# A fused attention, expert and gating kernel: lower weight halves a step later, masks ahead of ranks, last rows stored from ScalarE's queue

## The chip, the core and the metric

The kernel runs on one core of a Trainium2 chip. A core has TensorE (PE, matmuls; PEld is its weight load), VectorE (DVE), ScalarE (ACT), GpSimd (POOL) and SyncE (SP, which here only issues DMAs). ScalarE and GpSimd can issue DMAs too. Every engine works through its own list of instructions in order; semaphores hold an instruction until what it needs is there. The metric is the device time of one execution in microseconds (us), taken as the median of several runs; one more execution is profiled, and its trace is what the rows below come from.

## What is computed

Three layers follow one another: a linear attention with decay, a mixture of experts with one expert per token, and a gated projection. Cut to what matters:

```python
# attention, blocks of 64 positions, per head a decay lam
intra = (qb @ kb.T * Dmask) @ vb                  # Dmask[i, j] = lam ** (i - j) for i >= j, else 0
out   = intra + (qb * lam_pow) @ kv_state
kv_state = lam ** 64 * kv_state + (kb * rev_pow).T @ vb
# experts: x is [2, 768, 512]
for b, s:                                         # in order of s
    fresh = argmax(x[b, s] @ w_gate)
    e = fresh if s == 0 or sigmoid(x[b, s] @ w_local) < 0.5 else e_of_the_token_before
    p = softmax(x[b, s] @ w_gate)
    out[b, s] = p[e] * (relu(x[b, s] @ w1[e]) @ w2[e])
# gated projection: causal convolution of 5 taps, sigmoid gate
out = (sigmoid(conv(x)) * (x @ w_val)) @ w_out
```

## The kernel before, in words

There are 12 groups of 128 tokens (`NT`; 6 per batch entry) and 8 experts. The program has three parts.

**Attention and routing.** A loop over `s` from 2 to 11 pipelines four groups: `s`, `g1 = s-1`, `g2 = s-2`, `g3 = s-3`. In a step TensorE makes the scores of `s` (`scores`, L291), the attention output of `g1` (`mix_state` L309, `mix` L317), its next state (`next_state`, L346), then turns that output and multiplies it with the gate's weights (`turned`, L366 to L371); it also turns the expert choices of `g2` (`choice_turned` L427, `experts_turned` L439) and counts tokens per expert (`counted` L451, `counted_rest` L454, `indices` L469). VectorE masks the scores (`mask`, L298, two instructions), picks the expert (`logits` L376, `choice` L410 to L412), runs the scan along the tokens (`experts`, L435), ranks tokens within their expert (`ranks` L458, `index_factors` L463), and makes queries, states and half of the scaled keys. ScalarE copies the attention output (`mixed`, L323), the gate results (`token_rows`, L382 and L384), scaled keys (`keys`, L271), the one-hot rows (`one_hots`, L444 to L446), and at the end of a group its softmax (`softmax`, L420); after it the group's token rows (128 rows of 520 numbers, `xtok`) are stored to the DRAM table `xd` (L421).

In the same loop expert 0's first weights are prepared. A float32 weight tile is split into two parts that TensorE multiplies in its faster float32 form: the upper half is a cast on ScalarE (`split_hi`, L177), the lower half is the raw tile less the upper half on VectorE (`split_lo`, L181). `first_load(n)` (L171) loads raw tile `n` on SP's queue; `first_hi` and `first_lo` split half a tile (512 columns) per step, tiles 0 to 3 in steps 4 to 11. The raw tiles share four buffers, so that a load waits until the split of an older tile is done.

**The attention's end.** After the loop the last groups (`ge` = 9, `g0` = 10, `g1` = 11) go through the same steps; rows of expert 0 are not fetched from DRAM for these groups but placed by matmuls with one-hot tiles (`places` L494, `place` L502, from `xs`, the split token rows: `parts_hi` L388, `parts_lo` L391), after earlier groups' rows were gathered (`early_fetch` L482) and turned (`early_turn` L489). `early_split` (L511, L512) splits the result for expert 0.

**Experts and projection.** For each expert, `up` (L803) makes the hidden layer and `down` (L815) the output of each half of its tokens; `w1_chunk` and `w2_chunk` load and split weights ahead. The rows of expert 1 and later are gathered from `xd` by GpSimd (`x_fetch`, L759) by an index list `idx` (L672) and turned by TensorE between the two `down` calls of the expert before (`x_turn`, L779). A small gather of softmax values for expert 0 (`softmax_fetch`, L769) stands ahead of the first `x_fetch`. Every gather reads `xd`, so it needs all the stores that came before it. The gated projection follows (L1009, L1035).

The order on ScalarE, VectorE, TensorE and SP is the order in which the code is written; only GpSimd's is left to the scheduler in the first two parts. So where a call stands in the loop says where its instructions, and its DMA, stand on each queue.

Of the kernel before, what the change touches and what calls it, by code (L numbers as in the profile page):

```python
# [21 lines left out]
P = 128  # L22
# [20 lines left out]
def fused_kernel(ctx, tc, qkv, lam, wgl, w1, w2, wv, cw, wo, out, dbg=None):  # L43
# [282 lines left out]
    def decay(g):  # L326
        if 0 < g % NC < NC - 1:
            sd_t[g] = sd = at_p.tile([P, HP, D], F32, name="sdec", tag="sdec")
            for hp in range(HP):
                nc.scalar.activation(sd[:, hp, :], state[g][:, hp, :], AF.Copy, scale=lq[:, hp, P - 1:P])  # L330
# [83 lines left out]
    def inverse(g):  # L414
        den = ex_t[g][1]
        nc.vector.reciprocal(den[:, 1:2], den[:, 1:2])

    def softmax(g):
        (ex, den), xtok = ex_t.pop(g), xtok_t[g]
        nc.scalar.activation(xtok[:, DM:XW], ex, AF.Copy, scale=den[:, 1:2])  # L420
        nc.sync.dma_start(xd[1 + g * P:1 + (g + 1) * P, :], xtok)  # L421

    def choice_turned(g, b):
        fk = fk_t.pop(g)
# [96 lines left out]
    with tc.manual_schedule(engines=order_a):  # L521
        warm(10)
        scores(0, 0)
        scores(0, 1)
        mask(0)
        keys(0)
        load_qk(3)
        load_qk(4)
        scores(1, 0, True)
        scores(1, 1, True)  # L530
        mix_state(0)
        mix(0, 0)
        mix(0, 1)
        mixed(0)
        mask(1)
        keys_rest(0)
        powers()
        next_state(0)
        keep_state(0)
        queries(1)  # L540
        keys(1)
        keys_rest(1)
        scores(2, 0)
        turned(0)
        for s in range(2, NT):
            g1, g2, g3 = s - 1, s - 2, s - 3
            last = s == NT - 1
            if s < NT - 3:
                load_qk(s + 3)
            if s in (2, 4, 6, 8):  # L550
                first_load((s - 2) // 2)
            if s in (10, 11):
                first_load(s - 6)
            scores(s, 1)
            logits(g2)
            choice(g2)
            decay(g1)
            shift(g2)
            exponents(g2)
            token_rows(g2)  # L560
            if g3 >= 0:
                ranks(g3)
                index_factors(g3)
            mask(s)
            mix_state(g1)
            mix(g1, 0)
            mix(g1, 1)
            mixed(g1)
            if last:
                counted_rest(g3)  # L570
                indices(g3)
                early_fetch()
            next_state(g1)
            choice_turned(g2, g1)
            inverse(g2)
            queries(s)
            kept(g2)
            experts(g2)
            keep_state(g1)
            if not last:  # L580
                scores(s + 1, 0)
            turned(g1, (0, 1))
            experts_turned(g2)
            turned(g1, (2, 3))
            keys(s, range(2))
            one_hots(g2)
            keys_rest(s)
            keys(s, range(2, HK))
            softmax(g2)
            if last:  # L590
                parts_hi(g2)
            if s >= 4:
                first_hi((s - 4) // 2, HALF[s % 2])
                first_lo((s - 4) // 2, HALF[s % 2])
            if g3 >= 0 and not last:
                counted_rest(g3)
                indices(g3)
            counted(g2)

        ge, g0, g1 = NT - 3, NT - 2, NT - 1  # L600
        logits(g0)
        choice(g0)
        shift(g0)
        exponents(g0)
        token_rows(g0)
        parts_hi(g0)
        ranks(ge)
        places(ge)
        parts_lo(ge)
        mix_state(g1)  # L610
        mix(g1, 0)
        mix(g1, 1)
        mixed(g1)
        choice_turned(g0, g1)
        kept(g0)
        first_load(6)
        first_load(7)
        place(ge, (0,))
        parts_lo(g0)
        experts(g0)  # L620
        inverse(g0)
        turned(g1, (0, 1))
        experts_turned(g0)
        turned(g1, (2, 3))
        one_hots(g0)
        counted_rest(ge)
        counted(g0)
        place(ge, (1,))
        logits(g1)
        choice(g1)  # L630
        token_rows(g1)
        ranks(g0)
        places(g0)
        choice_turned(g1, NT)
        kept(g1)
        parts_hi(g1)
        experts(g1)
        place(g0)
        early_turn(0, (0, 1))
        experts_turned(g1)  # L640
        one_hots(g1)
        early_turn(0, (2, 3))
        counted_rest(g0)
        counted(g1)
        ranks(g1)
        places(g1)
        early_turn(1, (0, 1, 2, 3))
        parts_lo(g1)
        place(g1)
        shift(g1)  # L650
        exponents(g1)
        early_split()
        first_hi(4)
        index_factors(ge)
        index_factors(g0)
        index_factors(g1)
        inverse(g1)
        softmax(g0)
        softmax(g1)
        first_lo(4)  # L660
    idx = keep.tile([P, 2 * E], I32, name="idx")
    yslot = keep.tile([P, NT], I32, name="yslot")
# [581 lines left out]
```

## Time and profile before

| | us |
|---|---|
| runs: median of 3 (lowest, highest) | 357.74 (357.42, 358.5) |
| the profiled execution | 359.04 |
| its span, first to last instruction | 357.3 |
| busy in the span: TensorE, VectorE, ScalarE, GpSimd | 335.0, 260.5, 200.4, 66.4 |

The span is what the views cut into stretches; 1.74 us of the profiled execution lie around it. The profiled execution is 1.30 us above the median. Times in the rows count from the span's start. "Idle before" is how long an engine stood still ahead of an instruction, with what ended it. The chain of waits follows the work that ended last back to the start: at each step to what released it.

### The profile page before, as it was taken

The page shows a single profiled execution, that of the slowest core. Times are in us where ns is not written, and L with a number is a line of the kernel's source. Part 1 is how long each engine was busy: PE and PEld are TensorE (multiplying, and loading weights), DVE is VectorE, ACT ScalarE, POOL GpSimd, SP SyncE. Part 2 cuts the span into 40 slices and gives each one's busy share as a digit, 9 for nine tenths or more (in the row PEclk, how much of TensorE's full clock was granted, in tenths as well). Part 3 has the DMA queues.
Part 4 walks back from the last instruction along what each step waited for, and adds up shares of the span by engine and source line. Part 5 has one row for each costly group of instructions (what it writes and reads, how often), then busy time and mean ns, then how long its engine had stood idle before and what let it go on. Part 6 is the DMA issues. An engine that isn't in the chain of part 4 may idle for free.

```text
span 357.3 us, 6988 instructions
## 1 busy us (share of the span) xinstructions
PE 335.0 (94%) x2682; PEld 294.4 (82%) x2682; DVE 260.5 (73%) x540; ACT 200.4 (56%) x445; POOL 66.4 (19%) x89
## 2 busy tenths in 40 slices
PE   6999989979964999999999999999999999999995
PEld 2887867758943998989989889898898997999884
DVE  5777586856672788778898788776872399989880
ACT  1687577755443457564575655646552556655741
POOL 6000000020053304221241131421021263000000
PEclk9899899899996999999999999999999999999999
DMA  6988672530675778979969798797840262111012
GB/s 209 421 315 309 256 260 104 159 105 2 228 267 193 244 218 263 311 233 311 306 195 347 252 315 273 243 337 244 264 154 29 62 198 67 61 59 61 29 61 94
DMA packets 24819, 72.00 MB, mean 201 GB/s; under 512 B 3398, under 2 KB 6732, under 8 KB 23628
## 3 DMA queue, kind: packets, MB, share of 16 engines
q1 hardware_dynamic: 20020, 59.87, 49.2%
q0 software_dynamic: 2304, 7.42, 7.1%
q10 hardware_dynamic: 2456, 4.20, 3.1%
q8 instruction: 23, 0.38, 0.4%
q14 instruction: 16, 0.13, 0.1%
HBM read 57.79 MB, written 13.68 MB: 200 GB/s over the span
## 4 chain that ended last, share of the span: by engine, by line
PE 78%; DVE 7%; DMA 6%; ACT 4%; issue 1%; POOL 1%; SPq 0%; ACTq 0%; POOLq 0%; DVEq 0%
PE py L815 24%; PE ph L803 22%; PE po L1035 9%; PE pv L1009 7%; PE ps L291 3%; PE po L317 2%; DMA xr<-xd,idx 2%; PE rt L366 2%; DMA qk<-in_qkv_dram 2%; DMA xd<-xtok 2%; DVE sm L298 2%; DVE whl L181 1%; PE px L779 1%; DVE gt L995 1%; PE po L309 1%
## 5 line engine op out<-in xcount | busy, mean ns | idle before, releaser
L181 DVE TENSOR_TENSOR whl<-wraw,whl 128x1024 fp32r<-128x1024 f32 (+1 forms) x70 | 81.2, 1178 | 34.8 <-ACT whl L177 34.6
L815 PE MATMUL py<-whl,hh 128*128 128x512 f32 x384 | 93.8, 399 | 0.0
L803 PEld LDWEIGHTS ph<-xh,whl 128*128 128x128 f32 x768 | 87.3, 188 | 1.1 <-ACT xh L511 0.4
L803 PE MATMUL ph<-xh,whl 128*128 128x240 f32 x768 | 87.8, 275 | 0.2 <-ACT xh L511 0.2
L815 PEld LDWEIGHTS py<-whl,hh 128*128 128x128 f32 x384 | 71.5, 190 | 16.4
L177 ACT CAST whl<-wraw 128x1024 fp32r<-128x1024 f32 (+1 forms) x68 | 66.5, 995 | 9.2 <-DMA wraw<-in_w_dram 6.2
L806 ACT ACTIVATE hh<-ph 128x480 fp32r<-128x480 f32 x32 | 18.3, 572 | 39.2 <-PE ph L803 38.0
L995 DVE SCALAR_TENSOR_TENSOR gt<-yt,cw_sb,gt 128x256 f32<-128x256 f32 x96 | 39.0, 478 | 1.1 <-ACT gt L987 1.1
L1035 PE MATMUL po<-wo_t,gh 128*128 128x512 f32 (+1 forms) x156 | 34.6, 378 | 0.1
L1009 PEld LDWEIGHTS pv<-yh,wv_t 128*128 128x128 f32 x288 | 33.9, 188 | 0.6 <-ACT yh L972 0.2
L1009 PE MATMUL pv<-yh,wv_t 128*128 128x256 f32 x288 | 34.3, 278 | 0.0
L1035 PEld LDWEIGHTS po<-wo_t,gh 128*128 128x128 f32 x156 | 27.1, 188 | 6.0 <-DVE gh L1025 0.8
L807 DVE SCALAR_TENSOR_TENSOR hh<-ph,hh 128x480 fp32r<-128x480 f32 x32 | 21.0, 656 | 10.8 <-ACT hh L806 10.7
L291 PE MATMUL ps<-qk 64*128 64x128 f32 x176 | 19.1, 314 | 4.1 <-DVE sm L298 2.9
L822 ACT ACTIVATE yo<-py,pe 128x512 f32<-128x512 f32 x16 | 11.1, 695 | 19.1 <-PE py L815 19.1
L291 PEld LDWEIGHTS ps<-qk 64*128 64x128 f32 x176 | 13.8, 197 | 7.7 <-DVE sm L298 5.2
L759 POOL DMA_INDIRECT xr<-xd,idx x14 | 17.4, 1242 | 9.4 <-PE px L779 6.8
L271 ACT ACTIVATE kd<-qk,dm 128x64 f32<-128x64 f32 x40 | 11.4, 343 | 7.5 <-DMA qk<-in_qkv_dram 7.5
L317 PE MATMUL po<-sm,qk 128*64 128x128 f32 x192 | 15.0, 305 | 0.0
L951 POOL DMA_INDIRECT yg<-ys,yslot x10 | 11.6, 1163 | 15.9 <-DVE yh L974 11.1
L298 DVE TENSOR_TENSOR sm<-ps,dm 128x512 f32<-128x512 f32 x22 | 14.1, 682 | 0.2 <-PE ps L291 0.2
L317 PEld LDWEIGHTS po<-sm,qk 128*64 128x64 f32 x192 | 11.9, 154 | 2.4 <-issue 2.3
(172 smaller groups left out, 411.2 us busy)
## 6 DMA issues: line engine op xcount, KB each, us to landing
wraw<-in_w_dram SPq DMA_DIRECT2D x64, 512.0 KB, 5.9
qk<-in_qkv_dram SPq DMA_DIRECT2D x9, 1024.0 KB, 6.6
ys<-yo ACTq DMA_DIRECT2D x16, 256.0 KB, 6.0
xd<-xtok SPq DMA_DIRECT2D x12, 260.0 KB, 2.7
ys<-warm_sb SPq DMA_DIRECT2D x24, 128.0 KB, 5.5
out_dram<-oo SPq DMA_DIRECT2D x11, 256.0 KB, 2.0
qk<-in_qkv_dram SPq DMA_DIRECT2D x5, 512.0 KB, 8.1
wraw<-in_w_val_dram SPq DMA_DIRECT2D x4, 512.0 KB, 5.4
```

The lines of the kernel that those rows point to most:

```text
L177: nc.scalar.copy(hl[:, 0, cs], raw[:, cs])
L181: nc.vector.tensor_tensor(hl[:, 1, cs], raw[:, cs], hl[:, 0, cs].bitcast(F32), op=SUB)
L291: nc.tensor.matmul(ps_t[g][rh][:, hp, :], t[r, half, 256 + c0:256 + c0 + P], t[r, half, c0:c0 + P], start=True, stop=True)
L298: nc.vector.tensor_tensor(sm_t[g][:, rh], ps[rh], dm[:, rh * HP:(rh + 1) * HP, :], op=MUL)
L317: nc.tensor.matmul(po_t[g][hl * D:(hl + 1) * D, hp % 2, hp // 2 * P:(hp // 2 + 1) * P], qk_t[g][:, 3, h * D:(h + 1) * D], sm_t[g][:, h // ...
L803: nc.tensor.matmul(ph[:, fi, :], w1_t[e][k][:, a, f * P:(f + 1) * P], xh[:, b, k].rearrange("p t n -> p (t n)")[:, 0:C1], start=first, sto ...
L806: nc.scalar.activation(hh[:, 0, :, 0:C1], ph, AF.Relu)
L807: nc.vector.scalar_tensor_tensor(hh[:, 1, :, 0:C1], ph, 0.0, hh[:, 0, :, 0:C1].bitcast(F32), op0=ALU.max, op1=SUB)
L815: nc.tensor.matmul(py, hhs[f // 2][:, a, f % 2, t * P:(t + 1) * P], w2_t[e][f // 2][:, b, (f % 2) * DM:(f % 2 + 1) * DM], start=(n == 0), ...
L995: nc.vector.scalar_tensor_tensor(gt[:, k, :], yt[:, b, k, c0 + j:c0 + j + 256], cw_sb[:, k, j:j + 1], gt[:, k, :], op0=MUL, op1=ADD)
L1009: nc.tensor.matmul(pv[:, mi, :], wv_t[:, a, k * DM + m * P:k * DM + (m + 1) * P], yh[:, b, k, :], start=first, stop=last)
L1035: nc.tensor.matmul(po, gh[:, a, k, t * P:(t + 1) * P], wo_t[:, b, k * DM + cs.start:k * DM + cs.stop], start=(i == 0), stop=(i == 11))
```

## The change

Seven edits, all of place or queue; one line of the list of calls moves at a time, and the work itself is the same.

- In the loop the upper half of a tile is cast one step earlier (steps 3 to 10) and in the middle of the step, after `kept`; the lower half is subtracted where it was, so that it follows its upper half by a step.
- `keys(s, range(2))` comes before `experts` instead of after `turned`.
- `mask(s)` comes ahead of `ranks` and `index_factors` (except in the last step, where both come ahead of `mask`).
- `softmax` of a group, with its store, comes one step later and earlier within the step: `softmax(g3)` after `token_rows(g2)`.
- The stores of the last three groups (9, 10, 11) are issued by ScalarE, the others still by SP.
- In the attention's end `mix_state` and `mix` come ahead of the ranks, `parts_hi(g0)` comes after `kept` and `inverse`, `softmax(g0)` and `softmax(g1)` come much earlier, `parts_lo(g0)` and the placing of group 10 later and in two parts, the exponents of group 11 earlier.
- GpSimd's first gather for expert 1 comes ahead of the two small softmax gathers (the scheduler's choice).

```diff
-        nc.sync.dma_start(xd[1 + g * P:1 + (g + 1) * P, :], xtok)
+        (nc.scalar if g >= ET else nc.sync).dma_start(xd[1 + g * P:1 + (g + 1) * P, :], xtok)
...
             choice(g2)
+            if last:
+                ranks(g3)
+                index_factors(g3)
+            mask(s)
             decay(g1)
             shift(g2)
             exponents(g2)
             token_rows(g2)
             if g3 >= 0:
+                softmax(g3)
+            if g3 >= 0 and not last:
                 ranks(g3)
                 index_factors(g3)
-            mask(s)
             mix_state(g1)
...
             kept(g2)
+            if 3 <= s < 11:
+                first_hi((s - 3) // 2, HALF[(s - 3) % 2])
+            keys(s, range(2))
             experts(g2)
...
             turned(g1, (2, 3))
-            keys(s, range(2))
+            if last:
+                softmax(g2)
+                parts_hi(g2)
             one_hots(g2)
             keys_rest(s)
             keys(s, range(2, HK))
-            softmax(g2)
-            if last:
-                parts_hi(g2)
             if s >= 4:
-                first_hi((s - 4) // 2, HALF[s % 2])
                 first_lo((s - 4) // 2, HALF[s % 2])
...
         token_rows(g0)
-        parts_hi(g0)
+        mix_state(g1)
+        mix(g1, 0)
+        mix(g1, 1)
         ranks(ge)
...
         inverse(g0)
+        parts_hi(g0)
         turned(g1, (0, 1))
...
         counted(g0)
+        softmax(g0)
         place(ge, (1,))
...
         place(g1)
-        shift(g1)
-        exponents(g1)
+        inverse(g1)
+        softmax(g1)
         early_split()
         first_hi(4)
...
-        inverse(g1)
-        softmax(g0)
-        softmax(g1)
         first_lo(4)
```

On ScalarE, in one of the loop's full steps, from the copy of the attention output (`xt`) on, the list was:

```order
L323 COPY xt<-po 128x512
L431 ACTIVATE kp<-sp 8x128
L271 ACTIVATE kd<-qk,dm 128x64 x2
L444 CAST so_167<-sp 128x8
L445 COPY soall<-sp 128x8
L446 ACTIVATE so_167<-sp,tokid 128x8
L271 ACTIVATE kd<-qk,dm 128x64 x2
L420 ACTIVATE xtok<-ex,den 128x8
L177 CAST whl<-wraw 128x512
```

and in the same step it now is (`whl` is the split weight, `so_167` the one-hot rows, `kd` the scaled keys):

```order
L420 ACTIVATE xtok<-ex,den 128x8
L323 COPY xt<-po 128x512
L431 ACTIVATE kp<-sp 8x128
L177 CAST whl<-wraw 128x512
L271 ACTIVATE kd<-qk,dm 128x64 x2
L444 CAST so_167<-sp 128x8
L445 COPY soall<-sp 128x8
L446 ACTIVATE so_167<-sp,tokid 128x8
L271 ACTIVATE kd<-qk,dm 128x64 x2
```

The cast of the weight half moved from the step's last place to the middle, ahead of the one-hot rows, and the softmax from behind the keys to ahead of `xt`.

On ScalarE at the attention's end, from group 10's shift to the copy of group 11's attention output (`xt`) and beyond, the list was:

```order
L395 ACTIVATE nmx<-mx 128x1
L400 ACTIVATE ex,den<-rt,nmx 128x8
L401 ACTIVATE den<-den 128x1
L382 COPY xtok<-rt 128x256
L384 COPY xtok<-rt 128x256
L388 CAST xs<-xtok 128x512
L323 COPY xt<-po 128x512
L431 ACTIVATE kp<-sp 8x128
```

and now is:

```order
L384 COPY xtok<-rt 128x256
L323 COPY xt<-po 128x512
L431 ACTIVATE kp<-sp 8x128
L388 CAST xs<-xtok 128x512
L444 CAST so_167<-sp 128x8
L445 COPY soall<-sp 128x8
L446 ACTIVATE so_167<-sp,tokid 128x8
L420 ACTIVATE xtok<-ex,den 128x8
L421 DMA xd<-xtok 128x520
```

The split of group 10's rows (`xs`) went behind `xt` and `kp`, and the softmax with the store of `xtok` now stands here.

On SP's queue, around the two raw weight loads that stand ahead of the last stores, the difference is:

```order
 L421 DMA xd<-xtok 128x520
 L171 DMA wraw<-in_w_dram 128x1024 x2
-L421 DMA xd<-xtok 128x520 x2
 L215 DMA wraw_1595<-in_w_val_dram 128x1024
 L171 DMA wraw<-in_w_dram 128x1024 x4
```

The two stores of groups 10 and 11 no longer stand behind the two loads.

## Rows read from the trace of the kernel before

**Rows 1.** Stretches: busy PE, PEld, DVE, ACT, POOL; PE clock; DMA share; GB/s
```profile
24.85:29.95 5.10, 5.10 (x84) 4.38 (x81) 4.11 (x15) 4.31 (x21) 0.00 (x0) 1.00 0.69 215
29.95:67.53 37.58, 34.05 (x458) 28.16 (x455) 26.52 (x93) 26.60 (x116) 0.00 (x0) 0.95 0.61 221
67.53:74.03 6.50, 5.99 (x77) 4.84 (x74) 4.38 (x15) 4.48 (x22) 1.56 (x2) 0.77 0.46 127
74.03:86.53 12.50, 10.02 (x94) 8.10 (x92) 6.58 (x27) 7.01 (x28) 0.55 (x1) 1.00 0.20 63
86.53:103.40 16.87, 16.87 (x126) 15.39 (x126) 12.87 (x24) 8.38 (x13) 3.12 (x8) 1.00 0.61 211
103.40:119.20 15.80, 7.86 (x34) 6.37 (x33) 8.07 (x10) 5.22 (x7) 6.16 (x8) 0.78 0.66 215
119.20:357.30 238.10, 233.26 (x1574) 210.60 (x1572) 181.29 (x308) 131.82 (x196) 48.77 (x44) 1.00 0.59 193
```

**Rows 2.** Chain of waits through step 8: start, us, engine, what
```profile
48.84 0.19 ACT xtok L420
49.03 0.52 ACT whl L177
...
49.57 0.69 DVE whl L181
...
51.13 0.29 DVE ixa L463
51.42 1.21 DVE sm L298 x2
```

**Rows 3.** SP's first raw weight load; landing times of raw tiles, first 110 us
```profile
10.13 0.33 SPq L171 DMA_DIRECT2D wraw<-in_w_dram  x1
...
DMA to landing us min/median/max: 4.5/6.5/12.8
```

**Rows 4.** Timeline of VectorE as the attention's end begins: start, us, instruction, idle
```profile
75.10 0.69 DVE L181 TENSOR_TENSOR whl<-wraw,whl 128x512 fp32r<-128x512 f32 x1 [1.93 <-ACT whl L177]
```

**Rows 5.** Chain of waits at the attention's end
```profile
77.56 0.62 ACT xs L388
78.18 0.49 ACT xt L323
...
78.72 0.74 PE rt L366 x4
```

**Rows 6.** Timeline of ScalarE: a store that it issues itself
```profile
113.86 0.35 ACTq L824 DMA_DIRECT2D ys<-yo  x1
```

**Rows 7.** Timelines of ScalarE and SP around the last two stores
```profile
88.50 0.30 ACT L420 ACTIVATE xtok<-ex,den 128x8 f32<-128x8 f32 x1 [0.38 <-DVE den L416]
...
89.62 2.46 SPq L171 DMA_DIRECT2D wraw<-in_w_dram  x2
92.17 0.86 SPq L421 DMA_DIRECT2D xd<-xtok  x2
```

**Rows 8.** Chain of waits from the index list to expert 1's gathered rows
```profile
90.84 0.09 DVE idx L672
...
92.64 6.76 DMA xd<-xtok
...
100.18 0.95 POOL xsm L769
...
104.08 7.75 DMA xr<-xd,idx
```

**Rows 9.** All stores of token rows: landing times
```profile
DMA to landing us min/median/max: 2.1/2.7/6.8
```

**Rows 10.** Timeline of GpSimd: the second gather for expert 1
```profile
104.08 1.90 POOL L759 DMA_INDIRECT xr<-xd,idx  x1 [0.30 <-issue]
```

**Rows 11.** Timeline of TensorE, expert 1 to 2: turning, second half, next expert
```profile
135.54 0.79 PE L779 MATMUL px<-identr,xr 128*128 128x128 f32 x8
...
141.85 5.54 PE L803 MATMUL ph<-xh,whl 128*128 128x240 f32 x48
```

More of the change, by code (lines that the diff above doesn't have):

```diff
@@ L609, in fused_kernel @@
         parts_lo(ge)
-        mix_state(g1)
-        mix(g1, 0)
-        mix(g1, 1)
         mixed(g1)
@@ L618, in fused_kernel @@
         place(ge, (0,))
-        parts_lo(g0)
         experts(g0)
         inverse(g0)
+        parts_hi(g0)
         turned(g1, (0, 1))
@@ L633, in fused_kernel @@
         places(g0)
+        early_turn(0, (0, 1))
         choice_turned(g1, NT)
@@ L637, in fused_kernel @@
         experts(g1)
-        place(g0)
-        early_turn(0, (0, 1))
+        parts_lo(g0)
+        place(g0, (0,))
         experts_turned(g1)
         one_hots(g1)
+        shift(g1)
+        exponents(g1)
         early_turn(0, (2, 3))
@@ L644, in fused_kernel @@
         counted(g1)
+        place(g0, (1,))
         ranks(g1)
         places(g1)
+        parts_lo(g1)
         early_turn(1, (0, 1, 2, 3))
-        parts_lo(g1)
         place(g1)
-        shift(g1)
-        exponents(g1)
+        inverse(g1)
+        softmax(g1)
         early_split()
```

## The prediction

> **What bounds the kernel now.** I read the busy time of each stretch first, then the chain of waits inside the stretches where TensorE is not full, then the timelines around the places that the chain names. From 119.20 us to the end TensorE is busy 233.26 of 238.10 us [rows 1]: there the kernel is bound by matmuls, the change touches nothing, and whatever is won earlier should come out at the end whole. Expert 0 up to the end of its first `down` is full too (16.87 of 16.87). The stretches with holes are the six steps 5 to 10 (37.58 us, TensorE 34.05, with some of that stretched by matmuls that wait), step 11 (6.50), the attention's end (12.50, busy 10.02) and, the largest, 103.40 to 119.20, where TensorE works 7.86 of 15.80 us. The change works on exactly these four.
>
> **Steps 5 to 10.** In step 4, the last one without a weight split, TensorE is busy for 5.10 of 5.10 us [rows 1]. The next six take 37.58 / 6 = 6.26 us each. The chain shows why: it leaves TensorE and runs through ScalarE's softmax (0.19) and cast of the weight half (0.52) to VectorE's lower half (0.69), then the choice, the ranks and `ixa` (0.29) and the two masks (1.21), before TensorE may go on with the next scores [rows 2]. VectorE's next logits stand behind the lower half, which stands behind a cast that is the last thing ScalarE does in a step.
>
> With the change the lower half finds its upper half made a step earlier and waits for nothing; the softmax leaves this part of ScalarE's step; the masks no longer wait for ranks and `ixa`. What must still be done in a step is: TensorE 5.10 us, and in the six steps VectorE 26.52 / 6 = 4.42 and ScalarE 26.60 / 6 = 4.43 us [rows 1]. So TensorE should be last again, at 5.10. I take 5.30, since three engines that are each over 80% full hand work to each other in order: 6 x (6.26 - 5.30) = **5.8 us**. Ends: at 5.10 it is 7.0; if the three hold each other up and half of the 1.16 us between 6.26 and 5.10 stays, 5.68 a step, 3.5.
>
> The cast now stands ahead of the one-hot rows in ScalarE's list, and its 0.52 us are hidden as long as ScalarE's list does not reach past TensorE's: behind it wait two keys and the one-hot rows, for which `counted` on TensorE waits. It also needs its raw tile sooner. The load is issued at the start of step 2n+2 and cast about 2.9 us into step 2n+3, at 5.3 us a step some 8.2 us later; the landings are 4.5 to 12.8 us, median 6.5 [rows 3]. The 12.8 is tile 0's, issued at 10.13 into the crowd of first loads [rows 3]; it lands at 22.9, about when step 3 asks for it (a step of 5.1 us ahead of 24.85, and 2.9 into it: 22.7). SP is also freer now, as the stores of `xtok` stand earlier in each step. I charge **0.3** for waits on tiles (0 to 2).
>
> **Step 11.** It starts with the same wait of VectorE, and part of it ran at the lower of the clock's two levels, 1.2 GHz: a mean of 0.77 over 6.50 us is 3.0 us at half speed [rows 1]. At full clock TensorE's 5.99 us would be about 4.5. With a store and a row split now on ScalarE ahead of the one-hot rows I take 5.5 for the step: **1.0 saved** (0.5, to 1.4 at the 5.10 of step 4).
>
> **The attention's end.** VectorE begins it with 1.93 us of idle time, until 75.10, and then the lower half [rows 4]. Without the wait the lower half runs from 73.2 to 73.9, and the logits, at 75.7 before, follow TensorE's last turn, which is done when this stretch begins at 74.03: 1.6 us sooner. Next, `xt` stood behind the 0.62 us cast of `xs` and TensorE's turn waited for it [rows 5]; `xs` now comes after. 1.6 + 0.6 = **2.2 saved**. Against it: ScalarE now issues two stores inside this stretch, 0.35 us each by the nearest such issue [rows 6], plus two softmaxes of 0.30 [rows 7], and group 11's pair stands right ahead of the cast in `early_split` on which expert 0's start hangs. The first pair is covered by TensorE's placing; the second may cost up to 0.65. On the other side parts of the placing that stood in line go beside other work. Ends 1.0 and 2.9.
>
> **103.40 to 119.20.** The chain: `idx` is ready at 90.9, but GpSimd's gathers need all rows in `xd`. The softmaxes of groups 10 and 11 are the last things ScalarE does before expert 0, ending at 88.8; their stores stand on SP behind two raw loads that wait for buffers, and go out only at 92.17; they then take 6.76 us beside the weight loads [rows 7, 8], where the median store takes 2.7 [rows 9]. So gathers begin at 100.18 and the second of expert 1's lands at 111.83; only then can the second `down` run, part of it at the lower clock (0.78 over the stretch) [rows 1, 8].
>
> After the change both stores are out before expert 0 starts, into a stretch with a DMA share of 0.20 [rows 1]. Counted from the old clock, the gathers can begin when `idx` is there, at 91.0, 9.2 us earlier. Four issues at 0.95 to 1.90 us and 0.30 between them [rows 8, 10] put the last one's start between 94.8 and 97.6; with the 7.75 us of its landing taken whole it is there at 102.5 to 105.4. TensorE asks at 103.40. So the gap closes, to within 2 us at worst. What follows should look like the same place one expert later: from the turning at 135.54 to `up` at 141.85, 6.31 us [rows 11]. 15.80 - 6.31 = 9.5. Next late is the weight stream: expert 1's last raw tile waits for one of four buffers that VectorE frees only after it has converted a tile of the projection's weights. I keep 0.9 back for that and for the gather: **8.6 saved**. Ends: 9.5, and 5.5 if the gather is the full 2.0 late and a weight tile as much again.
>
> Here a rule speaks against the change. The Trainium skill (DMA: Bandwidth & Descriptors, section Issuing engines are not separate DMA queues) says that DMAs from ScalarE, SyncE and GpSimd run on the same 16 DMA engines and interleave, so that issuing from another engine saves only the issue time. By that rule alone the move of the stores would be worth the 0.86 us that SP's two issues took, and the gap would stay. The rows show another cost, though: 3.4 us in which the finished rows (88.8) stood behind other entries of SP's queue (92.17).
>
> **The sum.** 5.8 + 1.0 + 2.2 + 8.6 - 0.3 = 17.3 us. The profiled execution is 359.04 (357.3 of span and 1.74 around it), so its like would be 341.7. The median of the runs is 1.30 below the profiled execution; 357.74 - 17.3 = **340.4**, which I predict as the median.
>
> **Rivals.**
> 1. The gap closes in part only: the gather or expert 1's weights become the wait that ends last. For: a row [rows 10] shows an issue at twice its usual length beside a VectorE subtraction, and DMAs at 0.61 share in the stretch where the gathers now fall. Against: the last landing above, worst case 105.4. With the lower end of 5.5 saved: 340.4 + 3.1 = 343.5; another 2 us later on bring 345.5.
> 2. The steps stay bound by a round trip over ScalarE and VectorE, at 5.68 us: 2.3 us less won, 342.7. It is also what comes out if TensorE falls to the lower clock in a step that it now bounds, where before other engines set the pace: 3.0 us of it, as in step 11, cost 1.5.
> 3. The change does not do what it says, in that moving the queue brings only issue time: GpSimd still waits, on something the profile hides behind the stores. 340.4 + 8.6 - 0.9 = 348.1. That the chain runs from the store's landing at 99.40 to the gather at 100.18 [rows 8] speaks against it.
> 4. Slower. Steps that are shorter ask for the same bytes in less time; if the raw tiles then land late, the cast, which is now in the middle of ScalarE's list, holds the keys and one-hot rows behind it, and the step with them. A landing of L costs L - 8.2 for each of tiles 0 to 3. It eats the whole gain from L = 8.2 + 17.3 / 4 = 12.5; at 13.5 us the time is 340.4 + 4 x 5.3 = 361.6. Against: only one landing came near (12.8), while DMA moved 221 GB/s over these steps [rows 1], some 260 if they shrink as forecast.
>
> **How the numbers follow.** About 0.3% is what a measurement of this kernel can tell from no change, 1.1 us. Chances: forecast, 337 to 343, 0.66; rival 1, 0.16; rival 2, 0.10; rival 3, 0.04; rival 4, 0.03; better than 337, by the upper ends together (7.0 + 1.4 + 2.9 + 9.5 = 20.8, 336.9), 0.01. The range takes in the forecast, rival 2 and rival 1: 336.9 to 346.0. Faster 0.96, same 0.01, slower 0.03.
>
> **What would show it.** Right: scores of one step to the next some 5.3 us apart, with no idle VectorE ahead of the lower half; the two stores landed before the index list is ready; GpSimd's first gather starting right after `idx`; TensorE without a hole of more than 2 us between expert 0's `down` calls and a clock of 1.00 there. Wrong: ScalarE's cast waiting on a raw tile's landing; the gather landing over 2 us after the first `down` ends; TensorE idle inside expert 1 for its weights, which would mean that the gain was given back to the weight stream.

## The result

The changed kernel takes **341.59 us** (median of 4 runs, 339.49 to 342.98); the kernel before took 358.12 beside it (357.42 to 359.21). The ratio is 0.953, 95% interval 0.947 to 0.959. The time lies in the forecast range and close to the predicted number, but two of the terms behind that number were wrong, and they nearly cancelled. The profiled execution is the slowest of the four (342.98).

**The profile after, by stretch.** The windows view of the changed kernel, cut at the same places of the program as [rows 1] (step 4; steps 5 to 10; step 11; the attention's end; expert 0 to the end of its first `down`; from there to expert 1's `down`; the rest). Columns: window, its length, then busy time and number of instructions of each engine, the granted clock, the share of the DMA engines, and what they moved:

```profile
core 0: us, PE busy (x) PEld busy (x) DVE busy (x) ACT busy (x) POOL busy (x), PEclk, DMA share, GB/s
24.34:29.66 5.32, 5.10 (x84) 4.35 (x82) 4.71 (x16) 5.17 (x24) 0.00 (x0) 1.00 0.97 356
29.66:58.81 29.15, 28.89 (x458) 25.19 (x455) 26.87 (x94) 26.19 (x115) 0.00 (x0) 1.00 0.75 258
58.81:63.99 5.18, 4.67 (x76) 3.79 (x73) 4.38 (x16) 4.54 (x21) 0.00 (x0) 1.00 0.49 161
63.99:78.45 14.46, 11.98 (x94) 10.44 (x93) 5.99 (x27) 6.43 (x27) 2.19 (x3) 0.76 0.27 80
78.45:95.32 16.87, 16.87 (x129) 15.69 (x129) 12.20 (x22) 7.91 (x11) 6.07 (x11) 1.00 0.62 208
95.32:113.65 18.33, 17.43 (x129) 15.94 (x128) 17.37 (x20) 11.57 (x16) 9.05 (x6) 1.00 0.76 255
113.65:341.30 227.65, 222.52 (x1479) 199.95 (x1477) 174.37 (x299) 125.15 (x187) 45.02 (x41) 1.00 0.58 194
```

[rows 1] ends the fifth stretch where the second `down` could begin and starts expert 1 at 119.20; on the same cuts as here (expert 1's `down` at 129.95) the sixth stretch was 26.55 us:

```profile
103.40:129.95 26.55, 18.61 (x129) 17.11 (x129) 16.32 (x20) 11.82 (x16) 9.24 (x10) 0.87 0.65 208
```

Against [rows 1]:

| stretch | before | after | won | forecast |
|---|---|---|---|---|
| start, up to step 4 | 24.85 | 24.34 | 0.5 | - |
| step 4 | 5.10 | 5.32 | -0.2 | - |
| steps 5 to 10 | 37.58 | 29.15 | 8.4 | 5.8 |
| step 11 | 6.50 | 5.18 | 1.3 | 1.0 |
| attention's end | 12.50 | 14.46 | **-2.0** | **2.2** |
| expert 0 to its first `down` | 16.87 | 16.87 | 0 | 0 |
| from there to expert 1's `down` | 26.55 | 18.33 | 8.2 | 8.6 |
| rest | 227.35 | 227.65 | -0.3 | 0 |

The sum is 16.0, which is the difference of the two spans (357.3 and 341.3). In steps 5 to 10 TensorE is now busy for 28.89 of 29.15 us: the loop is bound by matmuls. The attention's end got longer, and its clock, 1.00 before, is 0.76.

**GpSimd.** Its timeline in the changed kernel; columns here and below are start, duration, engine, line, operation, and in brackets the idle time before it with what ended it:

```profile
66.74 1.16 POOL L482 DMA_INDIRECT xr<-xd,idx  x1 [56.66 <-ACT kp L431]
...
83.06 1.35 POOL L766 DMA_INDIRECT xr<-xd,idx  x1 [4.19 <-DVE rows L774]
84.72 1.42 POOL L776 DMA_INDIRECT xsm<-xd,rows  x1 [0.30 <-issue]
86.44 0.95 POOL L776 DMA_INDIRECT xsm<-xd,rows  x1 [0.31 <-issue]
87.70 1.23 POOL L766 DMA_INDIRECT xr<-xd,idx  x1 [0.30 <-issue]
...
94.80 0.20 POOL L795 COPY pe<-xr 128x2 f32<-128x2 f32 x1 [1.88 <-DMA xr<-xd,idx]
```

The first of the four gathers starts 0.3 us behind the index list (ready at 82.8), and the last of expert 1's rows land at 94.7, 7.0 us behind their issue and 0.5 ahead of their turning. Before, GpSimd stood 10.81 us for the stores and began at 100.18 [rows 8].

**TensorE.** The timeline of the changed kernel in the attention's end, and from the turning of expert 1's rows on:

```profile
67.85 0.71 PE L502 MATMUL px<-oh,xs 128*128 128x256 f32 x4
70.84 1.22 PE L489 MATMUL px<-ident,xr 128*128 128x128 f32 x4 [2.28 <-DMA xr<-xd,idx]
...
77.05 1.21 PE L502 MATMUL px<-oh,xs 128*128 128x256 f32 x8
78.45 2.96 PE L810 MATMUL ph<-xh,whl 128*128 128x240 f32 x24 [0.20 <-ACT xh L511]
...
95.16 0.80 PE L786 MATMUL px<-identr,xr 128*128 128x128 f32 x8
95.79 5.83 PE L822 MATMUL py<-whl,hh 128*128 128x512 f32 x24
101.46 1.79 PE L810 MATMUL ph<-xh,whl 128*128 128x240 f32 x11
104.02 1.17 PE L810 MATMUL ph<-xh,whl 128*128 128x240 f32 x8 [0.77 <-DVE whl L181]
```

In the kernel before, the same places were these:

```profile
82.76 0.61 PE L489 MATMUL px<-ident,xr 128*128 128x128 f32 x4
...
106.34 0.53 PE L779 MATMUL px<-identr,xr 128*128 128x128 f32 x4 [2.94 <-DMA xr<-xd,idx]
111.87 0.75 PE L779 MATMUL px<-identr,xr 128*128 128x128 f32 x4 [5.00 <-DMA xr<-xd,idx]
```

From 95.16 on expert 1's rows are turned without any wait, where TensorE had stood 2.94 and 5.00 us for them; a small wait for weights (0.77 us and stretched matmuls ahead of it) follows in expert 1. At 70.84 there is a new hole, a stretch in which TensorE has no work: the turning of expert 0's gathered rows waits 2.28 us for the early gather, and the four matmuls behind the wait take 1.22 us where at full clock they took 0.6.

### The profile page after: what moved, and what is told of

Read it like the earlier page. It is cut to its first block, busy times and chain, and to the rows that moved or that the text cites. A ratio compares the mean times of both kernels' runs of the same rounds, so it can differ in the third digit from the quotient of the medians.

```text
span 341.3 us, 6979 instructions
## 1 busy us (share of the span) xinstructions
PE 328.9 (96%) x2682; PEld 291.8 (86%) x2682; DVE 262.4 (77%) x540; ACT 199.7 (59%) x445; POOL 68.6 (20%) x89
## 4 chain that ended last, share of the span: by engine, by line
PE 77%; DMA 11%; DVE 6%; ACT 3%; issue 1%; SPq 0%; ACTq 0%; DVEq 0%
PE py L822 23%; PE ph L810 22%; PE po L1042 10%; DMA wraw<-in_w_dram 8%; PE pv L1016 8%; DMA qk<-in_qkv_dram 2%; PE ps L291 2%; PE po L317 2%; DVE gt L1002 1%; DMA xr<-xd,idx 1%; PE px L786 1%; PE px L489 1%; DVE whl L181 1%; PE po L309 1%; PE rt L366 1%; PE rt L369 1%
## 5 line engine op out<-in xcount | busy, mean ns | idle before, releaser
L181 DVE TENSOR_TENSOR whl<-wraw,whl 128x1024 fp32r<-128x1024 f32 (+1 forms) x70 | 84.3, 1222 | 21.2 <-ACT whl L177 21.0
L822 PE MATMUL py<-whl,hh 128*128 128x512 f32 x384 | 92.7, 396 | 0.0
L822 PEld LDWEIGHTS py<-whl,hh 128*128 128x128 f32 x384 | 70.7, 187 | 16.1
L766 POOL DMA_INDIRECT xr<-xd,idx x14 | 19.1, 1362 | 13.0 <-PE px L786 6.5
L271 ACT ACTIVATE kd<-qk,dm 128x64 f32<-128x64 f32 x40 | 11.5, 343 | 6.9 <-DMA qk<-in_qkv_dram 6.9
L291 PE MATMUL ps<-qk 64*128 64x128 f32 x176 | 15.5, 296 | 0.0
L958 POOL DMA_INDIRECT yg<-ys,yslot x10 | 11.5, 1153 | 15.9 <-DVE yh L981 11.2
L204 POOL TENSOR_TENSOR f64a<-f64a,f64s 128x512 f32<-128x512 f32 (+1 forms) x9 | 12.4, 1381 | 11.0 <-DVE f64s L203 10.7
L317 PE MATMUL po<-sm,qk 128*64 128x128 f32 x192 | 14.0, 291 | 0.0
L482 POOL DMA_INDIRECT xr<-xd,idx x2 | 2.1, 1052 | 57.0 <-ACT kp L431 56.7
```

What stands on the lines that cost most here:

```text
L181: nc.vector.tensor_tensor(hl[:, 1, cs], raw[:, cs], hl[:, 0, cs].bitcast(F32), op=SUB)
L291: nc.tensor.matmul(ps_t[g][rh][:, hp, :], t[r, half, 256 + c0:256 + c0 + P], t[r, half, c0:c0 + P], start=True, stop=True)
L317: nc.tensor.matmul(po_t[g][hl * D:(hl + 1) * D, hp % 2, hp // 2 * P:(hp // 2 + 1) * P], qk_t[g][:, 3, h * D:(h + 1) * D], sm_t[g][:, h // ...
L766: nc.gpsimd.indirect_dma_start(xr[:, t, :], None, xd, bass.IndirectOffsetOnAxis(ap=idx[:, 2 * e + t:2 * e + t + 1], axis=0))
L822: nc.tensor.matmul(py, hhs[f // 2][:, a, f % 2, t * P:(t + 1) * P], w2_t[e][f // 2][:, b, (f % 2) * DM:(f % 2 + 1) * DM], start=(n == 0), ...
```

## The experiments

Each is the changed kernel or the kernel before with one edit. The ratios are to the kernel before on the same chip, whose median was 357.97 beside four of them (store early, turning later, all stores on SP, queue edit alone), 362.36 beside the four on the loop, and 359.87 beside the other four; so ratios compare across the three sets, and times only within one. A ratio is taken as the record gives it; the quotient of the two medians differs from it by up to 0.3%. Windows rows are of one execution each, and those of different sets are of different chips.

### Why did the attention's end get longer?

The theory: the early gather reads the rows of groups 0 to 8. The change moved group 8's store from the end of step 10 into step 11, and so the gather is late.

**Store of group 8 early** (the changed kernel with this edit):

```diff
-            if g3 >= 0:
+            if g3 >= 0 and not last:
                 softmax(g3)
-            if g3 >= 0 and not last:
                 ranks(g3)
...
+            if s == NT - 2:
+                softmax(g2)
```

> The changed kernel, with one thing put back: group 8's softmax and store stand at the end of step 10 again, as they did before the change, instead of early in step 11. In the changed kernel the attention's end takes 14.46 us instead of the 12.50 of before; TensorE stands still for 2.3 us for the early gather, which needs this store, and the clock is low behind that hole. Theory (the late store makes the gather late, and the hole brings the clock down): the store goes out about 2.4 us earlier, the gather lands before TensorE asks, the hole is gone and the end takes 9.5 to 11 us, so 3.5 to 5 us less than the changed kernel in all, 337 to 338. Rival (the hole is only where another lateness shows: VectorE's and ScalarE's longer list in the end, with two stores issued by ScalarE): the stretch keeps 13.5 us or more and the time stays within 1 us of the changed kernel's 341.6.

Measured: 338.96 us, ratio 0.9463 (0.9419 to 0.9507). Its windows row of the attention's end, its TensorE timeline at the same place, and its GpSimd timeline:

```profile
63.90:73.56 9.66, 9.12 (x95) 7.89 (x93) 5.99 (x27) 6.43 (x27) 1.00 (x4) 1.00 0.31 97
```
```profile
67.75 0.72 PE L502 MATMUL px<-oh,xs 128*128 128x256 f32 x4
68.31 0.60 PE L489 MATMUL px<-ident,xr 128*128 128x128 f32 x4
```
```profile
62.24 1.16 POOL L482 DMA_INDIRECT xr<-xd,idx  x1 [52.14 <-ACT kp L431]
```

The hole is gone, the clock is 1.00, the stretch takes 9.66 us: 2.8 less than before the change and 4.8 less than after it. By the ratios the kernel gains only 2.4 us on the changed one, less than the 3.5 to 5 expected: the 14.46 us are of one execution, that of 342.98 us, and the median is 341.59. The other runs show the same order, with the hole where the gather is late. "Lands" is the last of the sixteen signals that a store sends:

| kernel | store of group 8 starts | lands after | gather starts | behind the landing |
|---|---|---|---|---|
| changed | 61.45 | 4.25 | 66.74 | 1.04 |
| changed, again | 60.90 | 3.77 | 65.71 | 1.04 |
| turn late | 61.05 | 3.81 | 65.91 | 1.04 |
| all stores on SP | 61.19 | 3.25 | 65.49 | 1.04 |
| masks late | 61.42 | 4.04 | 66.50 | 1.04 |
| hole filled | 61.31 | 3.69 | 66.05 | 1.04 |
| store early | 59.15 | 2.14 | 62.24 | 0.95 |
| before | 67.81 | 2.13 | 72.17 | 2.23 |

Only before the change is it clearly the index list that comes last (ready at 72.0, 0.2 us ahead of the gather). With the store early the list is ready at 61.9 and the store lands at 61.30, so either may be what the gather waits for. In the other runs the list was ready 3.7 to 4.7 us ahead of the gather, and the gather starts 1.04 us after the landing each time. The view names ScalarE as what ended GpSimd's idle time, at one of four instructions (`kp`, `xtok`, `ex`, `xt`) that differ from run to run, none of which the gather needs: the name is only that of the last event ahead of it. The trace also keeps the semaphores that GpSimd waits for. In the changed kernel its wait for that of group 8's store ends at 65.72, with the store's landing at 65.69; it has no wait for group 9's store, which lands later (66.39).

**Why the late store also lands late.** Moving the store took 2.4 us of the slack, its longer landing another 2.1. The DMA view of the changed kernel from 61 to 66 us (the first row has 40 slices of 0.125 us; `instruction` is the queue that brings in the program's own code):

```profile
GB/s 0 0 0 0 0 0 0 0 0 131 266 333 416 349 399 217 17 0 0 250 333 366 383 366 300 17 17 0 17 17 17 33 17 33 17 33 17 33 0 66
q8 instruction: 1, 0.02, 2.3%
xd<-xtok SPq DMA_DIRECT2D x1, 260.0 KB, 4.2
```

The stores of groups 8 and 9 pass in two bursts, but a trickle of 17 to 33 GB/s stays until 65.9. One packet of code takes 2.3% of 16 engines' 5 us, which is 1.84 us of one engine; in the trace's packets it runs from 62.23 to 64.09. Of the 128 rows of group 8, 120 are through by 63.09; the other 8, one engine's share of sixteen, start only as that packet ends, and the last is through at 65.14. Fifteen of the store's sixteen signals come by 63.48, the sixteenth at 65.69. All six runs of the table with a late store show this, and the longer the code packet, the later the landing: 1.27 us and 3.25 (all stores on SP), 1.42 and 3.77 (changed, again), 1.86 and 4.25 (changed). With the store early the code comes at 62.69, when the store has landed. So the store had moved under a code load. An estimate: with a landing of 2.14 us, and the 1.04 and 4.1 us to the gather's start and landing as here, the rows would be there at 68.7, against 68.56 when TensorE asked; nearly all of the hole would be gone. No run moves the code load alone.

**Turning later** (the changed kernel):

```diff
-        early_turn(0, (0, 1))
         choice_turned(g1, NT)
...
         place(g0, (0,))
+        early_turn(0, (0, 1))
```

> The changed kernel, with the first turning of gathered rows (two of four) put behind the first placing of group 10, where TensorE's list had it before; the store of group 8 stays late. Theory (TensorE stands still only because it asks for the gathered rows too early in its list): the other work fills the wait, the hole of 2.3 us shrinks to 1 us or less and the low clock behind it goes or is shorter; 1.5 to 4 us less than the changed kernel's 341.6. Rival (what stands between, the split rows of group 10 on VectorE, is late for another reason): the hole stays as long and moves to the placing; within 0.7 us of the changed kernel.

Measured: 340.14 us, 0.9492 (0.9446 to 0.9538). The end takes 10.97 us at a clock of 1.00; the hole has become 0.80 us, ahead of a later pair of turnings. The theory holds for the hole. By the ratios this wins 1.4 us on the changed kernel, with intervals that overlap: the weaker cure, since the gather is still late.

**The hole filled** (the changed kernel; nothing is changed in what is summed, zeros are added):

```diff
+        for _ in range(20):
+            nc.tensor.matmul(px0[0][:, 0, :], warm_sb[:, 0:P], warm_sb[:, 0:CAP], start=False, stop=False)
         early_turn(0, (0, 1))
```

> The changed kernel with one addition: ahead of the first turning of gathered rows in the attention's end, 20 matmuls of zeros by zeros (128x256, half precision), added to the same sums, so that TensorE works, some 2 us long, while the gather is on its way. Theory (the clock falls because TensorE stood still for 2.3 us): the clock stays at 1.00 in the attention's end, what follows the gather takes 5.2 us instead of 7.6, and the time is 1 to 2.5 us less than the changed kernel's, less where that ran at full clock anyway. Rival (the clock falls for another reason): clock of 0.8 or less in the end as before, and 0 to 0.5 us slower.

**The changed kernel again**, beside it:

> The changed kernel itself once more, beside the three others on the same chip: 0.953 of the time of before. What is asked of it is the difference to the others, and whether the clock in the attention's end falls in each execution.

Measured: with the hole filled 342.44 us, 0.951 (0.9473 to 0.9547); the changed kernel again 343.84 us, 0.9533 (0.9493 to 0.9573). Windows rows of the attention's end, first the one with the hole filled, then the changed kernel again, whose wait at the turning stands below it:

```profile
63.85:75.70 11.85, 11.30 (x114) 9.82 (x112) 5.98 (x27) 6.44 (x27) 2.35 (x5) 1.00 0.26 78
```
```profile
63.45:74.64 11.19, 9.45 (x94) 8.00 (x92) 5.98 (x27) 6.43 (x27) 2.27 (x4) 1.00 0.30 83
```
```profile
69.29 0.71 PE L489 MATMUL px<-ident,xr 128*128 128x128 f32 x4 [1.27 <-DMA xr<-xd,idx]
```

In this execution of the changed kernel the store landed sooner (3.77 us against 4.25), the hole was 1.27 us, the clock stayed at 1.00, and the end took 11.19 us: 1.3 less than before the change. The 14.46 us above belong to an execution with the longer hole. What follows the gather (from the turning to expert 0) takes 7.61 us at the low clock, 5.35 here and 5.24 with the hole filled: the low clock costs 2.3 us, in some executions. With the hole filled the clock stayed up, as the theory has it; but since it also stays up at times without, one execution of each doesn't prove the cause, and the intervals of the two times overlap. The mean clocks of the six whole runs of each point the same way, 0.981 to 0.995 for the changed kernel and 0.987 to 1.000 with the hole filled, but they don't tell where in a run the clock was low. That the hole brings the clock down is likely, not shown.

**Store of group 8 early, again**, on that chip:

> The first experiment once more (group 8's store early), beside the changed kernel on the same chip. Theory: 2.5 to 4.5 us less than the changed kernel there; rival: within 1 us of it.

Measured: 340.23 us, 0.9436 (0.9402 to 0.9471), 3.6 us less than the changed kernel beside it, with the ratios' intervals apart. This version beats both kernels.

### What closed the wait for expert 1's rows?

**All stores on SP** (the changed kernel) and **the queue edit alone** (the kernel before; here `+` and `-` are exchanged):

```diff
-        (nc.scalar if g >= ET else nc.sync).dma_start(xd[1 + g * P:1 + (g + 1) * P, :], xtok)
+        nc.sync.dma_start(xd[1 + g * P:1 + (g + 1) * P, :], xtok)
```

> The changed kernel, with one edit undone: all stores of token rows are issued by SP again. Theory (the gain of 8.2 us between expert 0's two down calls comes from the two last stores no longer standing behind weight loads that wait for buffers on SP's queue): the stores of groups 10 and 11 wait for the raw loads ahead of them (81.5 to 84 us in the changed kernel), the gathers begin 2 to 6 us later, TensorE stands still between the two down calls again, and the kernel is 3 to 8 us slower than the changed one, 344.5 to 349.5. Rival (the engine that issues a DMA saves only its issue time; the stores are earlier because the softmaxes are): 0 to 1 us slower, 341.6 to 342.6.

> The kernel before, with one edit of the change alone: the stores of the last three groups are issued by ScalarE, at the places where the softmaxes stood. Theory (the stores wait in SP's queue): they go out at about 88.2 and 89 us instead of 92.2 and 92.8, land some 3.5 to 5 us earlier, and the wait between expert 0's two down calls shrinks by as much; 352 to 354.5 in all (358.1 before). Rival (only the issue time is saved): 357 to 358. Third (both are needed: the softmaxes come so late that expert 0's weights share the DMA engines with the stores): 355 to 357.

Measured: all on SP 348.66 us, 0.9751 (0.9689 to 0.9813); the queue edit alone 352.11 us, 0.9814 (0.9755 to 0.9873). SP's queue and GpSimd with all stores on SP, and the windows row from the first `down` to expert 1's:

```profile
77.44 2.52 SPq L171 DMA_DIRECT2D wraw<-in_w_dram  x2
80.02 0.90 SPq L421 DMA_DIRECT2D xd<-xtok  x2
```
```profile
88.16 0.95 POOL L776 DMA_INDIRECT xsm<-xd,rows  x1 [13.31 <-DMA xd<-xtok]
```
```profile
91.29:118.08 26.79, 18.96 (x122) 17.16 (x122) 15.55 (x20) 11.89 (x16) 9.18 (x10) 0.81 0.61 200
```

The softmaxes are done by 73.6, yet the stores go out at 80.0, behind two raw loads that wait for buffers, and then land in 6.7 and 6.9 us. The stretch is 26.79 us again: the whole gain is lost, though the softmaxes stand early. With the queue edit alone, GpSimd's gathers and the same stretch:

```profile
95.81 0.95 POOL L759 DMA_INDIRECT xr<-xd,idx  x1 [5.68 <-DVE hh L807]
...
99.58 1.43 POOL L759 DMA_INDIRECT xr<-xd,idx  x1 [0.30 <-issue]
```
```profile
104.14:121.76 17.62, 17.09 (x130) 15.84 (x127) 15.42 (x19) 10.89 (x15) 7.84 (x7) 1.00 0.79 265
```

Here the softmaxes are as late as before and the stores (at 88.9 and 89.6) still share the DMA engines with weights, yet the stretch falls from 26.55 to 17.62. The last gather of expert 1 starts at 99.58 instead of 104.08 and lands in 5.3 us instead of 7.75 [rows 8], and that is enough. So the queue is the cause; the new place of the softmaxes adds nothing in this stretch (17.62 us, and 18.33 with all edits). The median wins less than the 8.9 us. In the profiled execution the attention's end is 1.5 us longer: ScalarE now issues group 9's store (0.35 us) ahead of two casts, VectorE waits 2.46 us for the second of them instead of 1.93, TensorE's first wait of the stretch grows from 0.62 to 1.16 us, and later in it the clock is low for 3.4 us (a mean of 0.88).

### What shortened the loop?

**The early cast alone** (the kernel before) and **the cast late again** (the changed kernel; `+` and `-` exchanged; `keys` stays where the change put it). What moves is the cast of the upper half; the lower half stays where it was:

```diff
             kept(g2)
+            if 3 <= s < 11:
+                first_hi((s - 3) // 2, HALF[(s - 3) % 2])
...
-                first_hi((s - 4) // 2, HALF[s % 2])
                 first_lo((s - 4) // 2, HALF[s % 2])
```

> The kernel before, with one edit of the change alone: ScalarE's cast of the upper weight half one step earlier and in the middle of the step, so that VectorE's lower half finds it made. Theory (the wait of VectorE for that cast is what made the six steps 6.26 us long): steps 5 to 10 fall to 5.0 to 5.3 us and step 11 by 1 us; the wait of TensorE for gathered rows between expert 0's two down calls stays, since the stores stay on SP's queue; 6.5 to 9 us less than before, 349 to 351.5. Rival (the masks behind the ranks bound the steps as well): steps at 5.6 us or more, 4 to 5 us less, 353 to 354.

> The changed kernel, with one edit undone: the cast of the upper weight half stands again at the end of the step right ahead of its lower half; the softmaxes stay away from it and the masks ahead of the ranks. Theory (the cast's place carries the loop's gain): steps 5 to 10 go back to 5.5 to 6.0 us from 4.86, so 4 to 7 us slower than the changed kernel, 345.5 to 348.5. Rival (with the softmax gone from ScalarE's end of step the cast is early enough where it is): within 1 us of the changed kernel's 341.6.

Measured: the early cast alone 352.19 us, 0.9694 (0.9624 to 0.9764), some 10 us less than the kernel beside it and so more than the 6.5 to 9 expected; the cast late 348.81 us, 0.9613 (0.9545 to 0.9682), some 3 us behind the changed kernel, less than the 4 to 7 expected.

**The masks first alone** (the kernel before) and **the masks late again** (the changed kernel; reversed): `mask(s)` ahead of `ranks(g3)` and `index_factors(g3)`, or behind them (in the last step `mask` stands behind them in both):

```diff
+            mask(s)
             decay(g1)
...
             if g3 >= 0:
                 ranks(g3)
                 index_factors(g3)
-            mask(s)
```

> The kernel before, with one edit of the change alone: the two masks come ahead of the ranks and their factors on VectorE. Theory (the masks stand behind the same wait for the cast, since the logits ahead of them do): the step gets shorter only by the ranks and factors that no longer stand between, some 0.3 to 0.5 us a step in those where they were in line, 0 to 3 us in all, 355 to 358. Rival (the masks are what the steps wait for, wherever the cast stands): 5 us or more less, below 353.

> The changed kernel, with one edit undone: the masks stand behind the ranks and their factors on VectorE again. Theory (with the cast out of the way TensorE sets the step, and VectorE has the room for this order): steps at 4.9 to 5.1 us, 0 to 1.5 us slower than the changed kernel's 341.6. Rival (masks are the last of what TensorE waits for in a step): steps at 5.2 us or more, 2 us or more slower.

Measured: the masks first alone 361.44 us, 0.9953 (0.9911 to 0.9994); the masks late 345.88 us, 0.9521 (0.9442 to 0.96). The windows rows of steps 5 to 10, of the early cast alone, the cast late, the masks first alone, and the masks late:

```profile
29.27:59.97 30.70, 29.76 (x459) 25.63 (x455) 27.08 (x94) 26.29 (x115) 0.00 (x0) 1.00 0.73 265
```
```profile
28.93:64.35 35.42, 32.52 (x458) 27.00 (x455) 26.51 (x93) 26.26 (x115) 0.00 (x0) 1.00 0.63 217
```
```profile
28.89:66.20 37.31, 33.95 (x458) 27.89 (x455) 26.52 (x93) 26.40 (x115) 0.00 (x0) 0.95 0.62 220
```
```profile
29.59:58.79 29.20, 29.20 (x459) 25.65 (x456) 26.88 (x94) 26.23 (x115) 0.00 (x0) 1.00 0.74 258
```

The early cast alone brings the six steps from 37.58 to 30.70 us, 6.9 of the 8.4. Taking it out of the changed kernel gives 6.3 back, and both rivals fall. The order of masks and ranks is worth 0.3 us alone and nothing in the changed kernel (29.20 against 29.15). The kernel with the cast late loses only those 3 us where its loop and step 11 lose 7.1: TensorE comes to the turning later there and finds the rows landed, and its attention's end takes 10.52 us instead of 14.46.

The early cast alone leaves the wait for expert 1's rows as it was:

```profile
65.15:76.08 10.93, 9.61 (x94) 8.10 (x92) 5.97 (x26) 6.38 (x27) 0.71 (x1) 1.00 0.26 73
92.95:119.00 26.05, 19.24 (x130) 17.61 (x129) 16.47 (x21) 11.98 (x16) 9.27 (x10) 0.87 0.67 213
```

and shortens the attention's end by 1.57 us (12.50 to 10.93), the part of the forecast that rested on VectorE's wait. Cast and queue together: 0.9694 x 0.9814 = 0.951, which is the whole change (0.953) within its interval. That the other edits add up to nothing is this product's reading, not a run's, and the traces speak against it: the attention's end takes 9.66 us with group 8's store early and 10.93 with the cast alone. So some of the other edits seem to win there, in those two executions, some of what the late store loses; no run separates them.

### Can the weight wait in expert 1 be taken away?

**Store early, and the projection's first tile behind expert 1's weights** (the first experiment, with this edit):

```diff
-                if e == 0 and j == 3:
-                    split64_a(0)
+                if e == 1 and j == 1:
+                    split64_b(0)
+                    split64_a(1)
...
-                if e == 0:
-                    split64_b(0)
-                split64_a(e + 1)
+                split64_a(e + 1 if e else 0)
```

> The changed kernel with group 8's softmax and store at the end of step 10 (as in the first experiment), and one more edit: the first tile of the projection's weights is loaded and converted behind expert 1's four weight tiles, and not ahead of them, and finished in the middle of expert 1. Theory (TensorE waits inside expert 1, 0.77 us and some stretched matmuls ahead of it, because expert 1's last raw tile waits for the buffer of that conversion): the tile is loaded some 3 us earlier, the wait goes, up of expert 1 starts without a hole, 1 to 2 us less than with the store alone: 0.942 of the time of before, 336.5 to 338 where that is 358. Rival (the tile lands when the DMA engines have carried the bytes, wherever it stands in the queue, or the conversion is missed later): no difference to the store alone, 0.946.

Measured: 341.26 us, 0.9474 (0.9441 to 0.9508), against 0.9436 for the store alone on that chip. A miss, and the trace shows where: TensorE's timeline in expert 1:

```profile
96.58 10.91 PE L811 MATMUL ph<-xh,whl 128*128 128x240 f32 x96
...
111.85 1.67 PE L823 MATMUL py<-whl,hh 128*128 128x512 f32 x6 [1.33 <-DVE whl L181]
114.09 1.43 PE L823 MATMUL py<-whl,hh 128*128 128x512 f32 x5 [0.57 <-DVE whl L181]
```

`up` of expert 1 indeed runs through, and its `down` begins 1.9 us sooner, counted from expert 0's `up`. But VectorE now converts the projection's second tile in the middle of expert 1 (106.09 to 110), the lower halves of expert 1's `w2` tiles stand behind it, and TensorE waits for those instead. The wait was moved and grew.

## Why the prediction was right, and where it wasn't

- **Steps 5 to 10: right mechanism, too small a term.** The wait for the cast was the bound, and TensorE took its place. The failed step is "at 5.10": one step's matmul time was taken for all six. The steps last 4.96, 4.56, 4.74, 4.91, 5.01 and 4.97 us. The second and third stand where one batch entry ends and the next begins; no next state is made in the one and no old state is read in the other. The 0.2 us a step kept for engines holding each other up did not appear. So 8.4 was won, above even the upper end of 7.0.
- **Waits on raw tiles: none in the loop.** The 0.3 charged falls away; step 4 grew by 0.2. Rivals 2 and 4 did not come.
- **Step 11: right**, 1.3 for 1.0, with the clock at 1.00.
- **The attention's end: wrong sign in the profiled execution.** The two gains were sized well: the early cast alone shortens the end by 1.57 us, where 1.6 was forecast for VectorE's wait, and with the store of group 8 at its old place the end is 2.8 us shorter, near the upper end of 2.9. The second pair of stores, for which up to 0.65 was allowed, cost nothing: ScalarE waits 1.36 us for TensorE behind it. The failed step is one that isn't in the working: the softmax of each group was moved, and the stores of groups 10 and 11 were followed to their readers, but not that of group 8, which the early gather needs. Before, it landed 2 us ahead of the index list (69.94 against 72.0), and TensorE turned the rows only at 82.76. The change used up that slack: the store comes 2.4 us later in step 11 and lands 2.1 us more slowly there, the index list comes 1.3 us sooner, and the turning stands ahead of the next group's choices. In the other profiled execution of the changed kernel, on another chip, the end took 11.19 us, 1.3 won: right in sign, and 0.9 short of the forecast.
- **The wait for expert 1's rows: right**, 8.2 for 8.6, and for the stated cause. The last gather landed 11.9 us after the index list, inside the 11.5 to 14.4 of the working; TensorE came 0.5 us later. Rival 3, that the queue edit brings only issue time, is refuted for this place: putting the stores back on SP costs the stretch 8.5 us (18.33 to 26.79). By the Trainium skill (DMA: Bandwidth & Descriptors, section Issuing engines are not separate DMA queues) another issuing engine saves only the issue time; the runs differ from it here, because the stores stood in line behind loads that waited. Whether it holds for transfers that are free to go, no run here shows.
- **What was named as next late** came: the weight stream, with 0.77 us of TensorE's idle time and slower first matmuls in expert 1 (`up` takes 12.2 us, 10.75 before: 1.4 us more), where 0.9 was kept back.

The profiled spans differ by 16.0 and the medians by 16.5, where 17.3 was forecast: 2.6 too little in the loop, 4.2 too much in the attention's end. The right total came out of two errors, and in part by luck: nothing in the working ties the one to the other.

## What to carry to other kernels

When a call moves, follow every DMA that it issues to all its readers, one by one; the slack of each is the time from its landing to the last of the other things its reader waits for. The landing may change with the place (here 2.1 and 4.2 us), so it is read again after the move. A store that a later part needs should not stand on a queue behind loads that wait for buffers; what that costs is read from the time between the finished rows and their issue (6.4 us with all stores on SP), not from the issue itself (0.9 us for both). Size the bound after a change from the instructions of each step, not from one step.

## What the runs showed of the hardware

- TensorE's clock in the attention's end, beside the wait ahead of the turning: after 2.28 us (the changed kernel) and 1.70 us (masks late) without work the matmuls that follow run at 1.2 GHz and the stretch's mean is 0.76 in both; after 1.27 us (the changed kernel again), 0.94 (all stores on SP) and 0.80 (turning late) it stays at 2.4 GHz, 1.00. A hole of one extra microsecond thus cost over three: 14.46 against 11.19 us. So two executions of the same kernel differ by more than the hole.
- The same store of 128 rows lands in 2.1 us when it is issued at the end of step 10 (59.2) and in 3.3 to 4.2 us when it is issued 2 us later, in step 11. There a 16 KB packet of the program's code occupies one DMA engine for 1.27 to 1.86 us, and that engine's sixteenth of the rows follows only behind it. Which engine a packet runs on, the trace doesn't say; the 8 late rows of 128 and the times say that it is one.
- A 128x1024 lower half on VectorE has a median of 1.22 us, but the one at 97.4 us takes 2.31, and the longest 2.35. The runs don't show why.
